# The last batch's first expert layer as plain products, and the kernel's last product in two column halves

## The chip, the core and the metric

The kernel runs on one core of a Trainium2 chip. The metric is device time in microseconds (us). The engines are PE (matrix products; its weight loads are listed as PEld), DVE (vector), ACT (scalar), POOL and SP, which issues most of the transfers. Products are added up in PSUM; GpSimd (POOL) does not touch PSUM here, so what it works on has first been moved to SBUF by DVE or ACT.

## The reference

Sinkhorn attention over 4 batches of 8 heads (768 tokens, head width 64, 8 blocks of 96 tokens) feeds a merged expert layer with 4 experts.

```python
P = sort_net                                   # (batch, head, 8, 8)
for _ in range(5):
    P = P - max(P, -1); P = exp(P); P /= sum(P, -1); P /= sum(P, -2)
k_sorted, v_sorted = P @ blocks of k, P @ blocks of v
attn = softmax(q_b @ k_sb.T / 8)               # inside each block of 96 tokens
x = (attn @ v_sb) laid out as (3072 tokens, 512)

p = domain_probs / sum(domain_probs, -1)       # (3072, 4)
for e in range(4):
    h = relu(x @ w1[e])                        # w1: 512 x 1024
    out += p[:, e] * (h @ w2[e])               # w2: 1024 x 512
```

## The kernel before

The program is written out for one core in a fixed order (`manual_schedule`): each engine's instructions stand in the order in which the lines below issue them, and semaphores are put in from the reads and writes of tiles. The four batches are worked off one after the other. While the expert layers of batch b run on PE, the attention stages of batch b + 1 (`st_q`, `st_v`, `st_k`, `st_s`, `st_a`, `st_x`) are put between them: `slot()` is called after each block of products, and a table (`PLAN`, L602; `PLAN0` for batch 0) says which stage goes into which slot of which chunk.

A batch has 768 tokens, worked on in 3 chunks of 256 (two tiles of 128 tokens). Each chunk has two layers.

- First layer, plain form (`chunk_first`, L733): for each of 4 experts and 2 halves of the 1024 hidden columns, 16 products with 256 token columns (4 output blocks by 4 contraction blocks) fill one PSUM tile of 128 x 1024. One DVE instruction (L748) takes the relu, multiplies by the expert weight `pb` and writes `Hb`. Between these, `h_sums` (L720, additions at L725 to L731) forms sums of blocks of `Hb` in `Sb` on DVE.
- Second layer (`chunk`, L757): seven block products p1 to p7 instead of eight, each 16 products with 256 columns over all experts (`product`, L771). They are read out on ACT and DVE and added on DVE and POOL into the tiles `oa` and `ob`, which SP stores to `out`. The product p3 comes last (L810, then the store of `oa`).

In the batch 3, which is the last, the first layer has another form in the kernel before. `last_chunk` (L1037) takes the place of `chunk`. For each expert, `seven` (L970) forms seven block products with 128 token columns, of 8 matmuls each (`product`, L978 to L981), with partial sums kept in PSUM banks X, Z and Q. It needs sums of weight blocks (`input_sums`, L913; 16 DVE instructions at L919, put into slots of batch 2 by `PLAN_A`, L1122), sums of token blocks (`token_sums`, L923; L935), ACT copies out of PSUM (L1001, L1008, L1016), a relu on ACT (L993) with a multiplication on POOL (L994), and DVE additions (L1017, L1025, L987). Blocks of the next chunk's first expert (`last_begin`, L1032) are put beside the last products of the chunk before. `last_banks` (L939) closes the two PSUM pools of the earlier batches, opens new ones, and issues one 512-column product (L948) on each occasion.

To make room for the weight sums, the attention inputs, the two spread matrices and `vo` lie in one tile, `arena` (L100), of which views are used; the temporary tiles of `seven` lie in buffers that the attention no longer needs.

At the end of the last chunk, p7 is read out by DVE (L1111), POOL and DVE complete `ob` (L1112, L1113), SP stores `ob` (L1114), DVE adds p3 (L1115), and SP stores the last half of `oa` (L1117). The first half of `oa` was stored earlier, after p2 (L1093).

Of the kernel before, what the change touches and what calls it, by code (L numbers as in the profile page):

```python
# [9 lines left out]
F32 = mybir.dt.float32  # L10
# [7 lines left out]
def kernel(  # L18
# [11 lines left out]
    nc = tc.nc  # L30
# [26 lines left out]

    openM, openA = [ctx.enter_context(ExitStack()) for _ in range(2)]
    psM = openM.enter_context(tc.tile_pool(name="psM", bufs=2, space=bass.MemoryType.PSUM))
    psA = openA.enter_context(tc.tile_pool(name="psA", bufs=2, space=bass.MemoryType.PSUM, side="right"))  # L60
# [36 lines left out]

    NW = 4 * R * D
    NQ = NPB * R * 2 * D
    arena = const.tile([P, 4 * NW + NQ + 4 * 4 * P + R * 4 * VW], F16, name="arena")  # L100

# [3 lines left out]
    def load_natural(b, nm, qd):  # L105
        src = {"k": k, "v": v}[nm]
        t = arena[:, ds(("k", "v").index(nm) * 2 * NW + qd * NW, NW)].rearrange("p (h r d) -> p h r d", h=4, r=R)
        natural[(b, nm, qd)] = t
        nc.gpsimd.dma_start(
            t.rearrange("p h r d -> p h (r d)"),  # L110
            src[b, ds(4 * qd, 4)].rearrange("h (p r) d -> p h (r d)", r=R),
        )

    def load_queries(b, heads=range(H)):

        if (b, "q") not in natural:
            natural[(b, "q")] = arena[:, ds(4 * NW, NQ)].rearrange("p (n t h d) -> p n t h d", n=NPB, t=R, h=2)
        t = natural[(b, "q")]
        for h in heads:
            nc.gpsimd.dma_start(t[:, h // 2, :, h % 2, :], q[b, h].rearrange("(t p) d -> p t d", p=P))  # L120
# [64 lines left out]
    kTs, ETs, vs0s, wide = [], [], [], []  # L185
# [4 lines left out]
    for n in range(4):  # L190
        ET = const.tile([P, S + 32], F16, name=f"ET_{n}")
        nc.gpsimd.memset(ET[0:BLK, ds(S, 32)], 0.0)
        ETs.append(ET[0:BLK])
        wide.append(ET)
# [4 lines left out]
    vo = arena[:, ds(4 * NW + NQ + 4 * 4 * P, R * 4 * VW)].rearrange("p (r h w) -> p r h w", r=R, h=4)  # L199
# [122 lines left out]
    def build_PI(eng, n, which):  # L322
        r4 = Rs[:, ds(4 * n, 4), :]
        if which == "k":
            PIk[n] = arena[:, ds(4 * NW + NQ + n % 2 * 4 * P, 4 * P)].rearrange("p (g i c) -> p g i c", g=4, i=NB)
# [6 lines left out]
        else:  # L332
            PIv[n] = arena[:, ds(4 * NW + NQ + (2 + n % 2) * 4 * P, 4 * P)].rearrange("p (g c i) -> p g c i", g=4, i=NB)
# [15 lines left out]
    def st_v(b, pr):  # L349
# [13 lines left out]
        if pr % 2:  # L363
            qd = pr // 2
            vs = att.tile([P, NB, 4, VW], F16, name=f"vs_{b}_{qd}", tag="vs")[0:BLK]
# [63 lines left out]
    def st_a(b, pr):  # L429
        xsl = att.tile([P, NB, 2, D], F16, name=f"xsl_{b}_{pr}", tag="xsl")[0:BLK]  # L430
# [109 lines left out]
    def h_a(qd, qq, ps=None):  # L540
# [11 lines left out]
        if qq not in xsls0:  # L552
            xsls0[qq] = att.tile([P, 2, 4, 2, D], F16, name=f"xsl0_{qq}", tag="xsl")[0:BLK]
# [203 lines left out]
    def chunk(b, c, slot, done=()):  # L757
# [7 lines left out]
        nxt = (b, c + 1) if c + 1 < R // 2 else (b + 1, 0)  # L765
        pbs[nxt] = load_p(*nxt)
# [4 lines left out]
        def product(n, lhs, rhs, pool=psm):  # L771
            ps = pool([P, DH], F32, f"ps_{n}_{b}_{c}")
            for e in es:
                if pool is last_bank and e == 2:
                    last["e0"][6]()
# [15 lines left out]
        if b:  # L791
# [5 lines left out]
            slot()  # L797
            nc.scalar.copy(p5[:], product("p5", sm(0), "t1"))
# [11 lines left out]
            tt(oa2, product("p3", sm(3), "b22", last_bank if last else psm), oa2, ALU.add)  # L810
# [26 lines left out]
        def last_adds(u3):  # L837
            gtt(ob2, u3, ob2, ALU.add)
            tt(ob1, ob1, u3, ALU.add)
# [4 lines left out]
        if c == 0:  # L844
# [21 lines left out]
            last_adds(u3[:])  # L866
            f4()
            store(1, ob)
        else:
# [18 lines left out]
            last_adds(u3[:])  # L888
# [4 lines left out]

    AW = 2 * KH * P

    def a_block(n):
        return arena[:, ds(n * AW, AW)].rearrange("p (k f) -> p k f", k=2)  # L900


    A_ORDER = (3, 4, 5, 10, 11, 0, 1, 2, 6, 7, 8, 9)
    As = []
    for e in range(E):
        w, hk, hf = w1sb[e], NKC // 2, FF // 2
        As.append({
            "a11": w[:, 0:hk, 0:hf], "a12": w[:, hk:NKC, 0:hf],
            "a21": w[:, 0:hk, hf:FF], "a22": w[:, hk:NKC, hf:FF], "s4": w[:, 0:hk, hf:FF],
            "s1": a_block(A_ORDER[3 * e]), "s3": a_block(A_ORDER[3 * e + 1]), "s2": a_block(A_ORDER[3 * e + 2]),  # L910
        })

    def input_sums(e, n):  # L913
        a = As[e]
        dst, x, y, op = (
            ("s1", "a21", "a22", ALU.add), ("s3", "a11", "a21", ALU.subtract),
            ("s2", "s1", "a11", ALU.subtract), ("s4", "a12", "s2", ALU.subtract),
        )[n]
        nc.vector.tensor_tensor(a[dst], a[x], a[y], op)  # L919

    Bs = {}

    def token_sums(c):  # L923

        b = B - 1
        xT = xTs[b].rearrange("p k i x -> p k (i x)")
        blk = lambda k, t: xT[:, ds(2 * k, 2), ds((2 * c + t) * P, P)]
        t3 = kTs[c % 2][:, 0:3 * 2 * P].rearrange("p (n k x) -> p n k x", n=3, k=2)
        t = Bs[c] = {
            "b11": blk(0, 0), "b12": blk(0, 1), "b21": blk(1, 0), "b22": blk(1, 1),  # L930
            "t1": t3[:, 0], "t2": t3[:, 1], "t3": t3[:, 2],
            "t4": wide[c % 2][:, 0:2 * P].rearrange("p (k x) -> p k x", k=2),
        }
        for dst, x, y in (("t1", "b12", "b11"), ("t2", "b22", "t1"), ("t3", "b22", "b12"), ("t4", "b21", "t2")):
            nc.vector.tensor_tensor(t[dst], t[x], t[y], ALU.subtract)  # L935

    last = {}

    def last_banks(n):  # L939

        (openA, openM)[n].close()
        pool = ctx.enter_context(tc.tile_pool(name=f"ps7_{n}", bufs=1, space=bass.MemoryType.PSUM, side=("right", "left")[n]))
        for nm, m in (("X", 1), ("Z", 1), ("Q", 2)):
            last[nm] = last.get(nm, []) + [
                pool.tile([P, 512], F32, tag=f"{nm}{i}", name=f"ps_{nm}{n}{i}") for i in range(m)
            ]

        nc.tensor.matmul(last["X"][n][:], w1sb[0][:, 0, 0:P], w1sb[0][:, 1, 0:512], start=True, stop=True)  # L948

    def prepare_last():  # L950

        last_banks(0)
        last["n"] = 1
        t = moe.tile([P, NKC, NB, BLK], F16, name="tmp7", tag="xT").rearrange("p k i x -> p (k i x)").bitcast(F32)
        room = [t[:, ds(n * 512, 512)] for n in range(3)]
        for m in range(2):
            t = att.tile([P, NB, 4, VW], F16, name=f"tmp7_{m}", tag="vs").rearrange("p i h w -> p (i h w)")
            t = t[:, 0:2048].bitcast(F32)
            room += [t[:, 0:512], t[:, 512:1024]]
        t = att.tile([P, NB, 2, D], F16, name="tmp7_2", tag="xsl").rearrange("p i h d -> p (i h d)").bitcast(F32)  # L960
        room.append(t)
        for n, nm in enumerate(("u2", "u3", "t22", "t12")):
            last[nm] = room[2 * n:2 * n + 2]

    def last_bank(shape, dtype, name):
        n = last["n"]
        last["n"] += 1
        return last["Q"][2 - n % 2][:, 0:shape[1]]

    def seven(c, e):  # L970

        b = B - 1
        a, t, pb = As[e], Bs[c], pbs[(b, c)]
        X, Z, u2, u3, t22, t12 = [last[nm][e % 2] for nm in ("X", "Z", "u2", "u3", "t22", "t12")]
        X, Z, Q = X[:], Z[:], last["Q"][e][:]
        tt = nc.vector.tensor_tensor

        def product(dst, lhs, rhs, first=False):  # L978
            for f in range(KH):
                for k in range(2):  # L980
                    nc.tensor.matmul(  # L981
                        dst[:, ds(f * P, P)], a[lhs][:, k, ds(f * P, P)], t[rhs][:, k, :],
                        start=(first and f == 0 and k == 0), stop=(f == KH - 1 and k == 1), skip_group_check=True,
                    )

        def finish(i, j, src):
            nc.vector.scalar_tensor_tensor(  # L987
                out=Hb[:, e, ds(i * KH, KH), ds(j * P, P)], in0=src.rearrange("p (f x) -> p f x", f=KH), scalar=0.0,
                op0=ALU.max, in1=pb[:, ds(e, 1), ds(j * P, P)].broadcast_to([P, KH, P]), op1=ALU.mult,
            )  # L990

        def finish2(i, j, src):
            nc.scalar.activation(src, src, AF.Relu, bias=0.0, scale=1.0)  # L993
            nc.gpsimd.tensor_tensor(  # L994
                Hb[:, e, ds(i * KH, KH), ds(j * P, P)], src.rearrange("p (f x) -> p f x", f=KH),
                pb[:, ds(e, 1), ds(j * P, P)].broadcast_to([P, KH, P]), ALU.mult,
            )

        def p1():
            product(Z, "a11", "b11", True)  # L1000
            nc.scalar.copy(X, Z)  # L1001

        def p5():
            product(Q, "s1", "t1", True)

        def p6():
            product(X, "s2", "t2")
            nc.scalar.copy(u2, X)  # L1008
# [287 lines left out]
```

## Time and profile before

| what | value |
|---|---|
| median of 3 runs | 369.53 us (369.51 to 370.15) |
| the profiled execution's own time | 369.51 us |
| its span (first to last instruction) | 367.7 us |
| outside the span | 1.81 us |
| PE busy | 358.5 us, 97% |
| DVE busy | 277.5 us, 75% |
| ACT and POOL busy | 121.5 and 118.6 us |
| granted TensorE clock | 1.0 |

Busy time of PE counts a matmul from its start to its modelled end. Matmuls overlap in that count, so the time that one takes in a stream is read from the starts of a row of equal ones and not from the mean duration. In the timeline, a line merges instructions that follow each other: start, length, engine, line, operation, tiles and shape, count, and in brackets the idle time before it and what ended it.

### The profile page before, as it was taken

The page shows a single profiled execution, that of the slowest core. Times are in us where ns is not written, and L with a number is a line of the kernel's source. Part 1 is how long each engine was busy: PE and PEld are TensorE (multiplying, and loading weights), DVE is VectorE, ACT ScalarE, POOL GpSimd, SP SyncE. Part 2 cuts the span into 40 slices and gives each one's busy share as a digit, 9 for nine tenths or more (in the row PEclk, how much of TensorE's full clock was granted, in tenths as well). Part 3 has the DMA queues.
Part 4 walks back from the last instruction along what each step waited for, and adds up shares of the span by engine and source line. Part 5 has one row for each costly group of instructions (what it writes and reads, how often), then busy time and mean ns, then how long its engine had stood idle before and what let it go on. Part 6 is the DMA issues. An engine that isn't in the chain of part 4 may idle for free.

```text
span 367.7 us, 9859 instructions
## 1 busy us (share of the span) xinstructions
PE 358.5 (97%) x4229; PEld 313.8 (85%) x4229; DVE 277.5 (75%) x521; ACT 121.5 (33%) x217; POOL 118.6 (32%) x146
## 2 busy tenths in 40 slices
PE   8799999999999999999999999999999999999996
PEld 8685858879889888898898888998888998998985
DVE  5654898766888774696695685698899879789695
ACT  2664330444230334222100235322011381561740
POOL 8872101713836403000921000100200283282471
PEclk9999999999999999999999999999999999999999
DMA  8999999996996768832795223604204102102101
GB/s 115 207 207 230 209 209 198 199 167 101 175 191 133 107 96 106 170 59 66 109 58 79 87 61 64 152 10 80 78 2 81 58 3 59 59 2 60 60 17 43
DMA packets 69752, 38.31 MB, mean 104 GB/s; under 512 B 40390, under 2 KB 64716, under 8 KB 69708
## 3 DMA queue, kind: packets, MB, share of 16 engines
q0 software_dynamic: 34640, 17.83, 37.3%
q1 hardware_dynamic: 35068, 19.85, 26.8%
q8 instruction: 33, 0.54, 0.6%
q14 instruction: 11, 0.09, 0.1%
HBM read 42.00 MB, written 6.34 MB: 131 GB/s over the span
## 4 chain that ended last, share of the span: by engine, by line
PE 80%; DMA 11%; DVE 5%; POOL 1%; issue 1%; ACT 1%; DVEq 0%; ACTq 0%
PE ps_h L742 28%; PE ps_p L777 23%; PE ps_Q L1069 8%; PE ps_X L981 4%; DMA w<-in_moe_w_dram 4%; DMA xT<-xsl 3%; PE ps_Q L981 3%; PE ps_Z L981 3%; PE ps_o L682 3%; DMA qT<-arena 2%; DMA arena<-in_q_dram 2%; PE ps_h L647 1%; PE ps_s L405 1%; DVE Sb L725 1%; PE ps_a L437 1%
## 5 line engine op out<-in xcount | busy, mean ns | idle before, releaser
L742 PE MATMUL ps_h<-xT,w 128*128 128x256 f16 x1056 | 121.0, 273 | 0.0
L742 PEld LDWEIGHTS <-w 128*128 128x128 f16 x1056 | 102.1, 98 | 13.1
L748 DVE SCALAR_TENSOR_TENSOR Hb<-ps_h,pb 128x1024 f16<-128x1024 f32 x66 | 80.7, 1223 | 29.5 <-PE ps_h L742 29.0
L777 PEld LDWEIGHTS <-Sb 128*128 128x128 f16 x528 | 50.9, 98 | 6.9 <-issue 0.3
L777 PEld LDWEIGHTS <-Hb 128*128 128x128 f16 x396 | 38.1, 98 | 4.6
L804 POOL TENSOR_TENSOR oa<-u,p 128x256 f32<-128x256 f32 x6 | 4.9, 809 | 103.9 <-issue 89.1
L994 POOL TENSOR_TENSOR Hb<-tmp,pb 128x512 f16<-128x512 f32 x24 | 30.9, 1293 | 20.2 <-ACT tmp L993 19.0
L395 ACT CAST kT<-ps_k 64x384 f16<-64x384 f32 x48 | 22.7, 473 | 38.2 <-PE ps_k L386 37.3
L412 ACT ACTIVATE ET<-ps_s 96x768 f16<-96x768 f32 x24 | 18.0, 802 | 46.2 <-PE ps_s L405 46.2
L777 PE MATMUL ps_p<-w,Hb 128*128 128x256 f16 x264 | 31.6, 273 | 0.0
L777 PE MATMUL ps_p<-T,Sb 128*128 128x256 f16 x264 | 31.1, 273 | 0.0
L777 PE MATMUL ps_p<-w,Sb 128*128 128x256 f16 x248 | 29.9, 273 | 0.1
L120 POOL DMA_DIRECT2D arena<-in_q_dram x24 | 19.9, 853 | 12.1 <-DMA w<-in_moe_w_dram 9.7
L981 PEld LDWEIGHTS <-w 128*128 128x128 f16 x384 | 23.3, 98 | 0.4
L725 DVE TENSOR_TENSOR Sb<-Hb 128x512 f16<-128x512 f16 x45 | 22.5, 511 | 0.0
L1069 PEld LDWEIGHTS <-Sb 128*128 128x128 f16 x192 | 18.3, 98 | 3.4 <-issue 0.9
L727 DVE TENSOR_TENSOR Sb<-Sb,Hb 128x512 f16<-128x512 f16 x45 | 18.3, 416 | 0.4
L729 DVE TENSOR_TENSOR Sb<-Hb 128x512 f16<-128x512 f16 x45 | 18.1, 418 | 0.0
L422 DVE TENSOR_TENSOR xsl<-ps_a,rz 96x512 f16<-96x512 f32 x24 | 16.5, 687 | 1.4 <-DMA xT<-xsl 0.6
L981 PEld LDWEIGHTS <-arena 128*128 128x128 f16 x288 | 17.4, 98 | 0.1
L731 DVE TENSOR_TENSOR Sb<-Hb,Sb 128x512 f16<-128x512 f16 x45 | 16.6, 425 | 0.0
L993 ACT ACTIVATE tmp<-tmp 128x512 f32<-128x512 f32 x24 | 15.2, 635 | 3.2 <-DVE tmp L1025 2.6
(173 smaller groups left out, 514.9 us busy)
## 6 DMA issues: line engine op xcount, KB each, us to landing
w<-in_moe_w_dram POOLq DMA_DIRECT2D x7, 1024.0 KB, 27.0
pb<-p_dram SPq DMA_DIRECT2D x12, 512.0 KB, 5.1
arena<-in_k_dram POOLq DMA_DIRECT2D x8, 384.0 KB, 7.9
arena<-in_v_dram POOLq DMA_DIRECT2D x8, 384.0 KB, 8.8
vs<-arena SPq DMA_DIRECT2D x36, 66.0 KB, 4.5
arena<-in_q_dram POOLq DMA_DIRECT2D x24, 96.0 KB, 6.5
out_dram<-ob SPq DMA_DIRECT2D x9, 256.0 KB, 2.2
out_dram<-oa SPq DMA_DIRECT2D x8, 256.0 KB, 2.3
```

Source lines behind the costliest of these rows:

```text
L120: nc.gpsimd.dma_start(t[:, h // 2, :, h % 2, :], q[b, h].rearrange("(t p) d -> p t d", p=P))
L395: nc.scalar.copy(kT[ds(D * hh, D), r], pk[ds(D * r, D), hh].rearrange("p a (i c) -> p a i c", c=CP),)
L412: nc.scalar.activation(ETs[2 * (pr % 2) + hh][:, 0:S].rearrange("c (a x) -> c a x", a=2), pss[hh][0:BLK, :, 0:HS], AF.Exp, bias=0.0, scale ...
L725: tt(sm[0], blk(0, 1), blk(1, 1), ALU.add)
L727: tt(sm[1], sm[0], blk(0, 0), ALU.subtract)
L729: tt(sm[2], blk(0, 0), blk(0, 1), ALU.subtract)
L742: nc.tensor.matmul(ps[:, f, :], w1sb[e][:, kc, ds((4 * g + f) * P, P)], xT[:, kc, ds(2 * c * P, 2 * P)], start=(kc == 0), stop=(kc == NKC ...
L748: nc.vector.scalar_tensor_tensor(out=Hb[:, e, ds(4 * g, 4), :], in0=ps[:], scalar=0.0, op0=ALU.max, in1=pb[:, ds(e, 1), :].broadcast_to([P ...
L777: nc.tensor.matmul(ps[:], lhs(e, f), Ts[e][rhs][:, f, :], start=(e == es[0] and f == 0), stop=(e == E - 1 and f == KH - 1),)
L981: nc.tensor.matmul(dst[:, ds(f * P, P)], a[lhs][:, k, ds(f * P, P)], t[rhs][:, k, :], start=(first and f == 0 and k == 0), stop=(f == KH - ...
L994: nc.gpsimd.tensor_tensor(Hb[:, e, ds(i * KH, KH), ds(j * P, P)], src.rearrange("p (f x) -> p f x", f=KH), pb[:, ds(e, 1), ds(j * P, P)].b ...
L1069: nc.tensor.matmul(ps, lhs(e, f), Ts[e][rhs][:, f, :], start=(e == 0 and f == 0), stop=(e == E - 1 and f == KH - 1),)
```

## The change

In the kernel after, the last batch goes through `chunk` like batches 1 and 2, without attention stages between, since no batch follows. `seven`, `last_chunk`, `input_sums`, `token_sums`, `last_banks`, `prepare_last`, `last_begin` and `PLAN_A` are gone, and with them `arena`: attention inputs, spread matrices and `vo` are tiles of their own again. The loads of batch 1's k, v and q are called some lines earlier in the program; on POOL they stand at the same place among the other instructions.

In the last chunk of the last batch, the first half of `oa` is stored after p2, as before. The last product p3 is formed in two halves of 128 output columns: 16 matmuls into a PSUM tile of the one pool, a DVE addition of 128 columns and a store issued by SP; then 16 matmuls into a tile of the other pool, a DVE addition and a store issued by ACT. The 128 KB store of the last half of `oa` becomes two of 64 KB.

```diff
-    openM, openA = [ctx.enter_context(ExitStack()) for _ in range(2)]
-    psM = openM.enter_context(tc.tile_pool(name="psM", bufs=2, space=bass.MemoryType.PSUM))
-    psA = openA.enter_context(tc.tile_pool(name="psA", bufs=2, space=bass.MemoryType.PSUM, side="right"))
+    psA = ctx.enter_context(tc.tile_pool(name="psA", bufs=2, space=bass.MemoryType.PSUM))
+    psM = ctx.enter_context(tc.tile_pool(name="psM", bufs=2, space=bass.MemoryType.PSUM))
+    nat = ctx.enter_context(tc.tile_pool(name="nat", bufs=2))
...
-    arena = const.tile([P, 4 * NW + NQ + 4 * 4 * P + R * 4 * VW], F16, name="arena")
...
-        t = arena[:, ds(("k", "v").index(nm) * 2 * NW + qd * NW, NW)].rearrange("p (h r d) -> p h r d", h=4, r=R)
+        t = nat.tile([P, 4, R, D], F16, name=f"nat_{nm}_{b}_{qd}", tag=f"nat_{nm}")
...
-            natural[(b, "q")] = arena[:, ds(4 * NW, NQ)].rearrange("p (n t h d) -> p n t h d", n=NPB, t=R, h=2)
+            natural[(b, "q")] = nat.tile([P, NPB, R, 2, D], F16, name=f"natq_{b}", tag="natq", bufs=1)
...
-        nxt = (b, c + 1) if c + 1 < R // 2 else (b + 1, 0)
-        pbs[nxt] = load_p(*nxt)
+        if (b, c) != (B - 1, R // 2 - 1):
+            nxt = (b, c + 1) if c + 1 < R // 2 else (b + 1, 0)
+            pbs[nxt] = load_p(*nxt)
...
+            parts = 2 if (b, c) == (B - 1, R // 2 - 1) else 1
+            if parts == 2:
+                nc.sync.dma_start(o[:, 2 * c, 0:DH], oa1)
             nc.scalar.copy(p5[:], product("p5", sm(0), "t1"))
...
             nc.sync.dma_start(o[:, 2 * c + 1, :], ob[:])
-            tt(oa2, product("p3", sm(3), "b22", last_bank if last else psm), oa2, ALU.add)
+            if parts == 2:
+                for n in range(2):
+                    ps = (psm, psa)[n]([P, DH // 2], F32, f"ps_p3_{b}_{c}_{n}")
+                    cols = ds(n * DH // 2, DH // 2)
+                    for e in es:
+                        for f in range(KH):
+                            nc.tensor.matmul(
+                                ps[:], sm(3)(e, f), Ts[e]["b22"][:, f, cols],
+                                start=(e == es[0] and f == 0), stop=(e == E - 1 and f == KH - 1),
+                            )
+                    tt(oa2[:, cols], ps[:], oa2[:, cols], ALU.add)
+                    eng = (nc.sync, nc.scalar)[n]
+                    eng.dma_start(o[:, 2 * c, ds(DH + n * DH // 2, DH // 2)], oa2[:, cols])
+                return
+            tt(oa2, product("p3", sm(3), "b22"), oa2, ALU.add)
...
-    def input_sums(e, n):
-    def token_sums(c):
-    def last_banks(n):
-    def prepare_last():
-    def seven(c, e):
-    def last_begin(c):
-    def last_chunk(c):
-    PLAN_A = [
...
     for b in range(B):
-        if b == B - 1:
-            for c in range(R // 2):
-                last_chunk(c)
-            break
         plan = PLAN if b else PLAN0
```

## The prediction, made before the changed kernel had run

> **What bounds the kernel now.** I read the page's head first, then the timeline of PE in the last two batches, then a table of stages, then DVE beside PE, and the end last.
>
> The page's head says that PE is busy nearly throughout, at the full granted clock, and that the chain that ended last is PE's.
>
> ```profile
> PE 358.5 (97%) x4229; PEld 313.8 (85%) x4229; DVE 277.5 (75%) x521; ACT 121.5 (33%) x217; POOL 118.6 (32%) x146
> PEclk9999999999999999999999999999999999999999
> PE 80%; DMA 11%; DVE 5%; POOL 1%; issue 1%; ACT 1%; DVEq 0%; ACTq 0%
> ```
>
> So the change is a matter of how many PE steps there are, how long one takes, and how long PE waits between them. The timeline of PE in batch 1 gives the step of a plain first-layer matmul (256 columns), that of batch 3 the step of a block product (128 columns).
>
> ```profile
> 151.18 7.15 PE L742 MATMUL ps_h<-xT,w 128*128 128x256 f16 x64
> 158.16 0.50 PE L386 MATMUL ps_k<-arena 128*128 128x128 f16 x6
> ...
> 316.29 0.61 PE L981 MATMUL ps_X<-kT,arena 128*128 128x128 f16 x8
> ...
> 325.67 1.47 PE L1069 MATMUL ps_Q<-w,Hb 128*128 128x256 f16 x12
> ```
>
> From 151.18 to 158.16 there are 64 steps: 6.98/64 = 109.06 ns. Between 316.29 and 325.67 the timeline has 21 groups of 8: 9.38/168 = 55.83 ns. A block product has half the columns and takes 51% of the time, although each has a weight load of its own.
>
> The table of stages has the stretch from and to, its length, then busy time (and count) of PE, PEld, DVE, ACT and POOL, clock, DMA. Rows one to three are the chunks of batch 1, four to six those of batch 2, seven to nine those of batch 3.
>
> ```profile
> 117.58:147.35 29.77, 29.77 (x311) 26.00 (x308) 20.48 (x34) 10.96 (x19) 8.73 (x10) 1.00 0.74 104
> 147.35:175.74 28.39, 28.39 (x302) 25.38 (x300) 21.02 (x38) 6.40 (x13) 2.47 (x4) 1.00 0.49 93
> 175.74:202.98 27.24, 27.24 (x274) 24.25 (x272) 19.36 (x34) 2.62 (x5) 11.99 (x14) 1.00 0.73 83
> 202.98:232.75 29.77, 29.77 (x311) 26.01 (x309) 19.62 (x35) 10.96 (x19) 1.71 (x2) 1.00 0.30 73
> 232.75:261.14 28.39, 28.39 (x303) 25.41 (x300) 23.92 (x44) 6.40 (x13) 1.51 (x3) 1.00 0.36 71
> 261.14:287.00 25.86, 25.86 (x259) 22.78 (x257) 23.25 (x42) 2.62 (x5) 1.31 (x2) 1.00 0.27 57
> 287.00:312.31 25.31, 25.21 (x340) 23.48 (x337) 21.21 (x43) 12.36 (x23) 12.06 (x11) 1.00 0.14 43
> 312.31:337.39 25.08, 24.93 (x338) 23.37 (x336) 20.93 (x42) 12.38 (x23) 11.81 (x11) 1.00 0.13 43
> 337.39:364.39 27.00, 26.85 (x354) 24.84 (x351) 21.75 (x42) 12.38 (x23) 12.83 (x12) 1.00 0.07 27
> ```
>
> The third row is the model of a chunk after the change: 240 plain steps are 240 x 0.10906 = 26.17 us, and the rest, 1.07, is the two attention stages in it (st_s 0.45, st_a 0.49) and 0.13 of gaps, most of it at st_s. In batch 3 these stages do not exist.
>
> **The change part by part.**
>
> *First layer of batch 3.* Removed are 3 chunks x 4 experts x 7 products x 8 = 672 steps of 55.83 ns, 37.52 us. Added are 3 x 128 = 384 steps of 109.06 ns, 41.88 us. On PE alone that is +4.36 us, all on the path, as PE's chain is the one that ends last.
>
> *What goes with the block products.* PE waits after p4 in each chunk of batch 3, for the late sums: 16 steps from 305.01 end at 306.76 and p5 starts at 307.02; the like from 330.06 to 332.11 and from 355.14 to 357.20. The three waits are 0.26 + 0.30 + 0.31 = 0.87 us. The two 512-column products at L948 take 0.21 us each by the starts around them, 0.42. I make the sum by whole stretches, so that small gaps count too. Before: from 261.14, the start of batch 2's last chunk, to 364.39, where p3 ends, is 103.25 us. After: that chunk as batch 1's, 27.24; three chunks of 26.17, 78.52; the drain of the last matmul behind its step, 0.16 as before (273 - 109 ns, 219 - 56 ns); and p3 in halves, 32 x 55.83 - 16 x 109.06 = 41 ns more. That is 105.96 us, so PE ends 2.71 us later. The terms named give 4.36 + 0.04 - 0.87 - 0.42 = 3.11; the 0.4 left are short gaps between the blocks and the DVE stall in the sixth row.
>
> *DVE in batch 2.* The 16 weight sums (L919, 0.68 us each, 10.9 us of DVE) and the token sums leave. Rows one and four, and two and five, are the same length to 0.01 us, with and without such sums; they lay beside PE and their removal is worth nothing there. Only the sixth row may have lost some 0.15 to them, which the stretch above contains.
>
> *Can DVE keep up with plain chunks without attention stages between?* The DVE timeline of batch 1's last chunk answers that. Each expert has two evictions (L748) and three block sums against 32 PE steps, 3.49 us.
>
> ```profile
> 183.48 1.23 DVE L748 SCALAR_TENSOR_TENSOR Hb<-ps_h,pb 128x1024 f16<-128x1024 f32 x1 [0.74 <-PE ps_h L742]
> 184.62 0.42 DVE L727 TENSOR_TENSOR Sb<-Sb,Hb 128x512 f16<-128x512 f16 x1
> 184.96 0.42 DVE L729 TENSOR_TENSOR Sb<-Hb 128x512 f16<-128x512 f16 x1
> 185.29 1.22 DVE L748 SCALAR_TENSOR_TENSOR Hb<-ps_h,pb 128x1024 f16<-128x1024 f32 x1
> 186.43 0.42 DVE L725 TENSOR_TENSOR Sb<-Hb 128x512 f16<-128x512 f16 x1
> ```
>
> From start to start an eviction with two sums takes 1.81 and one with one sum 1.14 + 0.33 = 1.47, together 3.28, and the next eviction (186.98) starts only when PE has finished its tile. An eviction is at most 0.07 late, and the tile has some 0.2 us to spare before PE wants it again. So I take no stall: 0, with 0.2 per chunk as the upper bound (the gap in the sixth row, 25.86 against 224 x 0.10906 + 0.94 + 0.21, is 0.28). In batch 3, POOL does nothing during the first layer, so it adds no contention. ACT's queue holds three copies per chunk. On SP, `load_p` stands as in batches 1 and 2, needed a second layer (12.2 us) later and landing in 5.1.
>
> *The end.* After p3 the path is: DVE addition, issue, landing, closing.
>
> ```profile
> 363.19 0.99 DVE L1113 TENSOR_TENSOR ob<-ob,u 128x256 f32<-128x256 f32 x1
> 364.25 0.33 SPq L1114 DMA_DIRECT2D out_dram<-ob  x1
> 364.50 0.42 DVE L1115 TENSOR_TENSOR oa<-ps_Q,oa 128x256 f32<-128x256 f32 x1 [0.30 <-PE ps_Q L1069]
> 364.95 0.33 SPq L1117 DMA_DIRECT2D out_dram<-oa  x1
> ```
>
> The addition of the first half can't start when its matmuls end, since DVE still works on `ob` (L1113) until some 0.2 us before p3 ends; the first half saves nothing by itself, and it is done, at about 364.5, as the second half's matmuls end. Its store stands behind that of `ob` on SP, 0.33, and nobody waits for it. The last addition has 128 columns: 256 take 0.42 and 512 take 0.69 (L1017), so 0.29 by the line through both, bounded by 0.20 (a reciprocal of 8 columns, L421) and 0.42. That saves 0.13. The last store moves to ACT, which has nothing queued behind and no DMA of its own in the trace: I take SP's 0.33, bounded above by SP's slow issues (0.58). It lands in 1.7 us at 128 KB, and the 8 KB load of `sort_net` also takes 1.7, so half the bytes save nothing; from 256 to 128 KB it fell from 2.0 to 1.7, so the bound is -0.3. The `ob` store goes out 0.7 before the last and lands 0.4 before it, so it does not take over. The end is worth -0.1, between -0.4 and +0.3.
>
> *Tiles instead of `arena`.* Instruction order is the same on every engine up to the last batch, sums apart. Waits differ in one place: the first query load of a batch waits for all transposes of the old queries instead of those of its own head. They are long done (at 96.77 seven of these loads go out without a pause). Worth 0; I allow 0.4 to either side, as the three runs of one program lie 0.64 us apart.
>
> **Sum.** 369.51 + 2.71 - 0.1 = 372.1 us. The profiled execution is 0.02 below the median, so no correction follows.
>
> **A rule against this.** In the trace a 128-column step with its weight load takes 55.83 ns. The Trainium skill (TensorE: Matmul & The Clock Gate, Back-to-back issue gap) says that a stream of pairs of weight load and matmul is paced by both, at about 81 ns for 128 columns. By that figure the 672 steps would have taken 54.4 us and their removal would make the kernel some 14 us faster (an estimate from that page). The measured step decides here.
>
> **The rivals.**
>
> - *DVE becomes the bound of the plain first layer.* By mean durations an expert costs DVE 2 x 1.223 + 3 x 0.418 = 3.70, against 3.49 on PE: 0.21 x 12 = 2.5 us more, 374.6 us. Against it speak the starts above, which overlap. Chance 0.08.
> - *Faster: the shared tile held up loads.* In the chain, DMA has 40 us: 1.7 and 14.7 at the head, and 24 between 69 and 99 us, through the load of q (L120) and two transposes. If separate tiles let loads of k, v and q start earlier, these parts could shrink; from 3.4 us on (2.6 lost and 0.74) the kernel gets faster. A quarter of the 16.4 at the head would give 372.1 - 4.1 = 368.0. Against it: the loads keep their place on POOL's queue, behind the weight loads that they wait for (9.7 and 8.5 us at L120 and L109), and between 69 and 99 us PE itself idles for them 0.85 and 0.47 us only. Chance 0.03.
> - *No difference.* If the halves at the end brought the whole landing forward (1.7 us) and the gaps another 0.3, some 370 us. The last bytes still leave after the last matmul. Chance 0.03.
>
> **How the numbers follow.** The forecast has 0.86. Its own ends: below, the end at -0.4 instead of -0.1 and the tiles at -0.4, which is 371.4; above, the end at +0.3 instead of -0.1 and three stalls of 0.2, which is 373.1. What is left out, 0.14, lies mostly above. About 0.2%, 0.74 us, can be told from no change here. Slower by that: 0.94; within it 0.03; faster 0.03.
>
> **What would show it.** Each chunk of batch 3 should take 26.2 us (between 26.1 and 26.4), with a step of 109 ns at the first layer's line, and no gap before p5. Batch 2's last chunk should take 27.2. The two last additions should be near 0.29 us each, the second store should come from ACT, and from the last matmul's end to the span's end it should be 3.2 us instead of 3.3. I am wrong if DVE's evictions show no idle time before them and PE waits at the first layer's line, or if batch 3 does not start at 288.4.

## The result, and the profile after

The kernel after takes 374.01 us (median of 4 executions, 373.49 to 375.28) against 369.52 us (median of 4), a ratio of 1.0125 with a 95% interval of 1.0095 to 1.0155. The direction was forecast. The time was not: it lies 1.9 us above the forecast and 0.9 us above the upper end of the range.

The profiled execution is the longest of the four, 375.28 us with a span of 373.4. First the page's head: PE's rows, its clock in 40 slices, and the shares of the chain that ended last.

```profile
PE 364.3 (98%) x3955; PEld 316.3 (85%) x3955; DVE 260.4 (70%) x470; ACT 87.8 (24%) x157; POOL 86.2 (23%) x122
PEclk9999999998999999999999999999999999999999
PE 87%; DMA 8%; POOL 2%; issue 1%; DVE 1%; ACT 0%; DVEq 0%; ACTq 0%; POOLq 0%
```

PE bounds the kernel still. One slice of the clock is below 9; it comes back further down. Next the table of stages, with the columns as in the prediction: the chunks of batches 1, 2 and 3.

```profile
120.37:150.13 29.76, 29.76 (x311) 26.00 (x309) 20.49 (x34) 10.97 (x19) 8.76 (x10) 1.00 0.71 107
150.13:178.52 28.39, 28.39 (x303) 25.39 (x300) 21.01 (x38) 6.41 (x13) 2.47 (x4) 1.00 0.50 91
178.52:205.76 27.24, 27.24 (x275) 24.26 (x273) 19.36 (x34) 2.62 (x5) 11.99 (x14) 1.00 0.69 83
205.76:235.52 29.76, 29.76 (x311) 26.01 (x309) 19.51 (x34) 10.97 (x19) 1.45 (x2) 1.00 0.27 73
235.52:263.91 28.39, 28.39 (x302) 25.39 (x300) 21.01 (x38) 6.41 (x13) 1.45 (x2) 1.00 0.30 71
263.91:291.15 27.24, 27.24 (x275) 24.25 (x272) 19.35 (x34) 2.62 (x5) 1.45 (x2) 1.00 0.26 54
291.15:317.35 26.20, 26.20 (x243) 23.48 (x240) 17.73 (x30) 1.12 (x3) 1.45 (x2) 1.00 0.12 42
317.35:343.55 26.20, 26.20 (x243) 23.48 (x240) 17.74 (x30) 1.12 (x3) 1.45 (x2) 1.00 0.12 41
343.55:369.95 26.40, 26.40 (x258) 23.70 (x255) 17.94 (x31) 1.12 (x3) 1.45 (x2) 1.00 0.07 26
```

From the start of batch 1 on, every row is as forecast: 27.24 for batch 2's last chunk, 26.20 for a chunk of batch 3, PE busy without a gap. From 263.91 to the end of p3 at 369.95 it is 106.04 us; forecast were 105.96, and 103.25 before. What was not forecast stands in the first number: batch 1 starts at 120.37 and not at 117.58. All that is before it is called the head here. By it batch 3 starts at 291.15 and not at 288.4, one of the prediction's signs of being wrong.

The end, from the timeline:

```profile
368.00 1.95 PE L813 MATMUL ps_p<-w,Sb 128*128 128x128 f16 x32
369.69 0.59 DVE L817 TENSOR_TENSOR oa<-ps_p,oa 128x128 f32<-128x128 f32 x2
369.83 0.33 SPq L805 DMA_DIRECT2D out_dram<-ob  x1
370.21 0.42 SPq L819 DMA_DIRECT2D out_dram<-oa  x1
370.36 0.37 ACTq L819 DMA_DIRECT2D out_dram<-oa  x1
```

The last addition takes 0.28, as forecast (0.29), but from the end of p3 to the end of the span it is 373.4 - 369.95 = 3.45 us; before it was 367.7 - 364.39 = 3.31.

So of the 5.7 us between the two spans 2.77 lie between batch 1's start and p3's end, 0.14 at the end, and 2.79 ahead of batch 1. In the head PE's timeline shows where a part of that is. Before:

```profile
82.19 0.51 PE L405 MATMUL ps_s<-qT,kT 64*128 64x96 f16 x16 [0.85 <-DMA qT<-arena]
82.64 1.92 PE L742 MATMUL ps_h<-xT,w 128*128 128x256 f16 x16
```

After:

```profile
83.90 0.51 PE L398 MATMUL ps_s<-qT,kT 64*128 64x96 f16 x16 [2.14 <-DMA qT<-natq]
84.35 2.79 PE L735 MATMUL ps_h<-xT,w 128*128 128x256 f16 x16
```

PE waits 2.14 us instead of 0.85 for the transposed queries of batch 1's second pair of heads, and the 16 first-layer products behind that wait take 2.79 us instead of 1.92. The row of the 3.4 us from 85.20 on has a granted clock of 0.50:

```profile
85.20:88.60 3.40, 3.40 (x30) 2.71 (x29) 1.43 (x2) 0.75 (x2) 0.00 (x0) 0.50 0.80 77
```

This slow stretch belongs to the execution that was profiled (its mean granted clock is 0.993, that of the other three 1.0). The later head is there without it too, as follows.

### The profile page after: what moved, and what is told of

Read it like the earlier page. It is cut to its first block, busy times and chain, and to the rows that moved or that the text cites. A ratio compares the mean times of both kernels' runs of the same rounds, so it can differ in the third digit from the quotient of the medians.

```text
span 373.4 us, 9110 instructions
## 1 busy us (share of the span) xinstructions
PE 364.3 (98%) x3955; PEld 316.3 (85%) x3955; DVE 260.4 (70%) x470; ACT 87.8 (24%) x157; POOL 86.2 (23%) x122
## 4 chain that ended last, share of the span: by engine, by line
PE 87%; DMA 8%; POOL 2%; issue 1%; DVE 1%; ACT 0%; DVEq 0%; ACTq 0%; POOLq 0%
PE ps_h L735 40%; PE ps_p L769 35%; DMA w<-in_moe_w_dram 4%; PE ps_o L675 3%; PE ps_h L640 3%; DMA qT<-natq 2%; DMA natq<-in_q_dram 2%; PE ps_a L430 2%; PE ps_s L398 1%; PE ps_k L379 1%; PE ps_v L346 1%; POOL nat_k L103 0%; POOL nat_v L103 0%; PE ps_s L522 0%; POOL oacc L845 0%
## 5 line engine op out<-in xcount | busy, mean ns | idle before, releaser
L735 PE MATMUL ps_h<-xT,w 128*128 128x256 f16 x1440 | 164.2, 273 | 0.0
L735 PEld LDWEIGHTS <-w 128*128 128x128 f16 x1440 | 140.1, 98 | 17.6
L741 DVE SCALAR_TENSOR_TENSOR Hb<-ps_h,pb 128x1024 f16<-128x1024 f32 x90 | 110.1, 1223 | 41.5 <-PE ps_h L735 39.9
L769 PEld LDWEIGHTS <-Hb 128*128 128x128 f16 x540 | 52.4, 98 | 6.3
L769 PE MATMUL ps_p<-w,Hb 128*128 128x256 f16 x360 | 43.5, 274 | 0.0
L769 PE MATMUL ps_p<-T,Sb 128*128 128x256 f16 x360 | 42.1, 273 | 0.0
L769 PE MATMUL ps_p<-w,Sb 128*128 128x256 f16 x344 | 41.3, 273 | 0.1
L114 POOL DMA_DIRECT2D natq<-in_q_dram x24 | 19.9, 852 | 12.4 <-DMA w<-in_moe_w_dram 9.9
L769 PE MATMUL ps_p<-T,Hb 128*128 128x256 f16 x180 | 21.6, 272 | 0.0
L352 ACT CAST vo<-ps_v 128x768 f16<-128x768 f32 x12 | 9.5, 801 | 20.2 <-PE ps_v L346 12.0
```

Source lines behind the costliest of these rows:

```text
L735: nc.tensor.matmul(ps[:, f, :], w1sb[e][:, kc, ds((4 * g + f) * P, P)], xT[:, kc, ds(2 * c * P, 2 * P)], start=(kc == 0), stop=(kc == NKC ...
L741: nc.vector.scalar_tensor_tensor(out=Hb[:, e, ds(4 * g, 4), :], in0=ps[:], scalar=0.0, op0=ALU.max, in1=pb[:, ds(e, 1), :].broadcast_to([P ...
L769: nc.tensor.matmul(ps[:], lhs(e, f), Ts[e][rhs][:, f, :], start=(e == es[0] and f == 0), stop=(e == E - 1 and f == KH - 1),)
```

## The experiments

Two theories stood at first. **T**: the separate tiles, which the prediction priced at nothing, make the head later. **P**: any kernel with a plain last batch has it (by the length or place of its program, or by the order of its transfers), whatever the tiles. A third possibility was chance: a profile is one execution. Each kernel below was timed beside the kernel before; times are medians in us, and the ratio is to the kernel before in the same series of executions.

| kernel | time (range, executions) | ratio (95%) | batch 1 starts in its profile |
|---|---|---|---|
| after, again | 374.67 (373.18 to 375.25, 6) | 1.0144 (1.0118 to 1.0170) | 118.53 |
| before, again | 369.57 (368.80 to 370.31, 12) | 0.9987 (0.9971 to 1.0003) | 117.48 |
| after, p3 whole | 374.22 (373.67 to 374.67, 5) | 1.0118 (1.0097 to 1.0139) | 119.05 |
| shared tile, plain last batch | 373.73 (372.03 to 374.05, 6) | 1.0099 (1.0077 to 1.0122) | 118.53 |
| the same, a second time | 372.62 (372.04 to 373.73, 6) | 1.0080 (1.0064 to 1.0095) | 117.01 |
| with work tiles of their own | 372.70 (371.93 to 374.28, 6) | 1.0076 (1.0062 to 1.0090) | 119.23 |
| with natural q, k, v of their own | 373.75 (372.82 to 375.51, 6) | 1.0116 (1.0095 to 1.0137) | 119.95 |
| with natural q of its own | 373.51 (373.44 to 375.20, 5) | 1.0115 (1.0084 to 1.0145) | 118.19 |
| with natural k, v of their own | 373.52 (372.18 to 374.61, 6) | 1.0097 (1.0064 to 1.0129) | 119.47 |
| after, a third time | 373.70 (372.88 to 374.54, 5) | 1.0109 (1.0092 to 1.0125) | 118.08 |

### Chance or program

The kernel after, unaltered:

> The changed kernel once more, unaltered. The last batch went as forecast (26.20 us a chunk); the excess of 1.4 to 3 us lies before 100 us, where the profile shows PE waiting 2.14 us at st_s for a q transpose (0.85 before) and one 3.4 us stretch at half clock after it. Theory T (the later head belongs to the new program: tiles in place of the shared arena move addresses and the timing of loads): 373.5 to 374.3 again, with PE's wait at st_s 1.7 us or more. Rival C (chance: both kernels' heads vary alike): some of the rounds fall to 372.0 to 372.5 and the wait at st_s in this profile is near 0.85.

And the kernel before, unaltered:

> The kernel before, unaltered, for a second profile of its head. Four profiles of plain last batches show PE waiting 1.7 to 2.2 us at st_s for the second q transpose, one of them with the head's instructions exactly those of before. Theory P (the head follows the whole program, such as where it lies in memory): the wait is near 0.85 again, landing of the q load 5.9 us after its issue and the transpose 7.1. Rival C (chance): the wait is 1.5 us or more in this profile too, and the time of that run is 370.2 or more.

374.67 and 369.57 us: the difference is the program's, not chance. But one profile of a head is worth little. The kernel before again, which needs no longer, shows a wait of 1.46 us at the same place, between what the two theories expected, and its times spread over 1.5 us.

The lowered clock comes back as well. Half clock over 3.4 of some 370 us makes a mean granted clock of 0.995 (an estimate from the row above). Of the 15 executions of the kernel after in all its series, four are at 0.993 to 0.995, with a mean of 375.14 us, and eleven at 1.0, with a mean of 373.75. Of the 72 executions of the kernel before beside these experiments, five are at 0.995 or less.

### The end: halves or whole

```diff
-            parts = 2 if (b, c) == (B - 1, R // 2 - 1) else 1
+            final = (b, c) == (B - 1, R // 2 - 1)
+            parts = 1
...
-            nc.sync.dma_start(o[:, 2 * c, :], oa[:])
+            if final:
+                nc.sync.dma_start(o[:, 2 * c, DH:Dm], oa2)
+            else:
+                nc.sync.dma_start(o[:, 2 * c, :], oa[:])
```

> The changed kernel with the last product undivided: 16 matmuls of 256 columns, one addition, one 128 KB store on SP. The prediction gives the halves 0.1 us, so 0.1 us slower than the changed kernel, between 0.4 slower and 0.3 faster. If the store on ACT were what costs the excess, this one would be 1 us or more faster.

374.22 us against 374.67 for the halves in the same series, and 3.37 us from the end of p3 to the end of the span against 3.47: the halves and the store from ACT bring nothing that can be measured. The end is not the cause of the miss.

### Where the queries are loaded

Since PE waits for transposed queries, three kernels moved their loads or transposes. The first loads the second pair of heads three slots earlier (in the kernel after):

```diff
-        (0, 9, st_v, 0), ... (0, 11, st_k, 0), (0, 11, st_n, 1), (1, 0, st_q, 1),
+        (0, 8, st_n, 1), (0, 9, st_v, 0), ... (0, 11, st_k, 0), (1, 0, st_q, 1),
```

> The changed kernel with the load of the second pair of q heads (st_n 1) three slots earlier, so that on POOL it stands ahead of the two additions that wait for ACT, some 5 us earlier. If PE's wait for the q transpose at st_s is what makes the head late, it goes (2.1 us in the profile of after, or 1.3 us more than before), and the kernel takes 371.7 to 372.4. If the load only queues longer behind the weight loads (DMA engines full until 72 us), the wait shrinks by less than 0.5 us and the time stays at 373.5 or more.

373.77 us (372.77 to 375.51), ratio 1.0112 (1.0086 to 1.0138): no gain that can be told from the spread, and not the 371.7 to 372.4 expected. In its profile the wait moves to the scores before, 2.75 us at 75.3, and 1.03 are left at 85.1.

The second takes load and transposes of the last pair out of the crowded stretch, in the kernel after and, for comparison, in the kernel before:

```diff
-        (1, 4, st_n, 3), ... (1, 9, st_q, 3),
+        (1, 7, st_n, 3), ... (2, 0, st_q, 3),
```

> The changed kernel with the last pair of q heads of batch 1 loaded later: on POOL behind the addition that waits for ACT at 87 us instead of at 73 to 75, its transpose moved from slot (1, 9) to (2, 0). If the second q transpose is late because four q loads run beside it (7.5 us in place of 3.7), it takes 6.5 us or less and PE's wait at st_s falls below 1.2 us: 372.2 to 373.2. If the load before it is what makes it late (6.5 us behind the weight loads), the wait stays at 1.7 or more and the time at 373.5 or more.

> The kernel before with the same later load of the last pair of q heads. The wait at st_s (0.85) goes if the four loads beside the transpose cause it: 368.4 to 369.0, faster than both kernels. If the moved transpose meets the load of the next batch's queries, which waits for it, 369.4 or a little more.

380.26 us (ratio 1.0256, 1.0226 to 1.0286) and 372.89 us (1.0077, 1.0047 to 1.0108). In the kernel after, with two query loads beside them instead of four, the transposes of the second pair landed in 5.8 us instead of 7.5, and the wait of 2.14 us fell to 0.55, so what runs beside these transfers changes when they land. But the moved transposes are then needed sooner than they land: in the first kernel PE waits 2.66 us at 105.7 and 4.29 at 124.1, in the second 3.16 at 106.8.

### The shared tile kept: a first, misleading answer

This kernel is the one before with the last batch in the plain form and nothing else: up to the last batch its instructions and tiles are those of the kernel before, apart from the weight and token sums and the first block products, which stood in batch 2.

```diff
-        if b == B - 1:
-            for c in range(R // 2):
-                last_chunk(c)
-            break
... (nor the calls of input_sums, prepare_last, token_sums and last_begin in batch 2, nor load_p after the last chunk)
```

> The kernel before with nothing changed but the last batch, which goes through the plain chunk; the shared arena, pools, places of loads and the undivided last product stay. Theory T: the head is that of before, so 372.1 to 372.4, 1.5 us or more below the changed kernel in the same rounds, PE's wait at st_s near 0.85. Rival C: the same as the changed kernel within 0.5 us. A third, D (the change of the last batch itself costs more in timed runs than in the profile): 373.5 or more with a head like before's.

373.73 us, and batch 1 at 118.53 in the profile. I read that as the end of theory T and looked for what any plain kernel shares. That reading was too quick: it rested on one profile and on six times spread from 372.03 to 374.05.

### The length of the program

The plain kernels' programs are shorter. Work behind the end, which no output uses, made the shared-tile kernel as long as the kernel before:

```diff
+    pool7 = psM.tile([P, 512], F32, tag="ps", name="pad_ps")
+    for _ in range(292):
+        nc.tensor.matmul(pool7[0:32, 0:32], ident[:, 0:32], ident[:, 0:32], start=True, stop=True)
... (and 73, 80 and 36 one-column fills or copies on DVE, ACT and POOL)
```

> The shared-arena kernel with the plain last batch, and behind its end 292 tiny products (32 columns), 80 one-element ACT copies, 73 DVE and 36 POOL memsets that compute nothing, so that each engine's program is as long as before's; they take some 8 to 20 us at the end, which is to be taken off. Theory P in the form that program length matters: the wait at st_s falls to near 0.85 and the last batch begins about 1 us earlier in the span than in the kernel without them. Rival C, or any cause other than length: the wait is again 1.7 or more.

Its profile had batch 1 at 117.55, as before; so the same was done to the kernel after (with 276 products), in full and in parts, and the kernel before was cut short:

```diff
-            for c in range(R // 2):
+            for c in range(R // 2 - 1):
                 last_chunk(c)
```

> The kernel after, with work behind its end that no output uses: 276 products of 32 x 32 on PE, 73 fills of one column on DVE, 80 one-column copies on ACT, 36 fills on POOL, so that every engine's program has about as many instructions as in the kernel before. Its time is not to be compared, only the start of batch 1's first chunk. Theory L (the length or place of the program in memory sets how the head runs): the head ends as in the kernel before, batch 1 starts at 117.4 to 117.9 us, with PE's wait before the scores of the second half near 1 us, and p3 ends near 366.9 to 367.3 (364.39 + 2.71). Theory C (the head is late for a cause in the changed kernel's own instructions, or by chance of the execution): batch 1 starts at 118.5 to 120.5, and p3 ends at 368 to 370.

> The kernel before without the last chunk of the last batch (rows 2816 to 3071 of the output are left out), which makes its PE program as short as that of the kernel after (7835 instructions instead of 8459; after 7911), while every engine's instructions up to there, and every address, are those of the kernel before. Theory L: batch 1 starts at 118.5 us or later, as in all three kernels with a short program. Theory C: batch 1 starts at 117.4 to 117.9, as in the kernel before. The time should be about 27.0 us (one chunk, 337.39 to 364.39) less than before: by L 343.5 to 346, by C 342.3 to 343.0.

> The kernel after with the 276 products of 32 x 32 on PE behind its end and nothing on the other engines. They take 276 x 25.5 ns = 7.0 us if they start as p3 ends; the store's 3.5 us lie beside them. If PE's program length alone decides (a part of theory L), batch 1 starts at 117.4 to 117.9 as in the kernel before; if the other engines' programs decide or nothing does, 118.5 to 120.5.

> The kernel after with the fills and copies on DVE, ACT and POOL behind its end and nothing on PE. If the length of these engines' programs decides, batch 1 starts at 117.4 to 117.9; if PE's does or nothing does, 118.5 to 120.5. ACT's 80 copies take some 16 us, so the time itself is 10 to 15 us longer.

The kernel after with all of it starts batch 1 at 118.45, with PE's alone at 121.22, with the rest alone at 120.15; the kernel before, cut, at 117.87, and the spans of its five executions (345.0 to 345.7) lie within 0.7 us. None of these profiles shows that the length of the program is it: the three padded forms of the kernel after keep a late head, and the cut kernel before has an early one. (The padded kernels' times, 383.08, 390.50, 380.40 and 390.86 us, hold the added work. The cut kernel's time, 347.21 us, misses both expectations: 337.39 is where the first products of the cut chunk begin, put between the last ones of the chunk before, whose p3 ends at 340.9 in the cut kernel's trace. That has no bearing on the head.)

### The tiles, settled by many executions

What was left was to time the shared-tile kernel again, in one series with the kernel after and two kernels between them. One has the natural q, k and v in tiles of their own (`nat`, as in the kernel after), the other the spread matrices, `vo` and the 96-row tiles. The edits, one for each kernel:

```diff
-        t = arena[:, ds(("k", "v").index(nm) * 2 * NW + qd * NW, NW)].rearrange("p (h r d) -> p h r d", h=4, r=R)
+        t = nat.tile([P, 4, R, D], F16, name=f"nat_{nm}_{b}_{qd}", tag=f"nat_{nm}")
...
-            natural[(b, "q")] = arena[:, ds(4 * NW, NQ)].rearrange("p (n t h d) -> p n t h d", n=NPB, t=R, h=2)
+            natural[(b, "q")] = nat.tile([P, NPB, R, 2, D], F16, name=f"natq_{b}", tag="natq", bufs=1)
```

```diff
-            PIk[n] = arena[:, ds(4 * NW + NQ + n % 2 * 4 * P, 4 * P)].rearrange("p (g i c) -> p g i c", g=4, i=NB)
+            PIk[n] = att.tile([P, 4, NB, CP], F16, name=f"PIk_{n}", tag="PIk")
... (the same for PIv; vo, ET, vs and xsl as in the kernel after)
```

> The plain last batch with the shared tile kept, unaltered a second time, beside the kernel after and two kernels between them, so that the four heads can be told apart by many executions and not by one profile each. Theory T (the tiles that replace the shared tile make the head later): its head is that of the kernel before, batch 1 starts at 117 to 118.5, and its time is 369.5 + 2.7 + 0.4 = 372.6 us (0.4 for the 256 KB store at the end), 372.0 to 373.2. Theory P (any kernel with a plain last batch has the late head): batch 1 starts at 118.5 to 120.5 and the time is 373.5 to 375.

> As the kernel with the shared tile, but the natural k, v and q of the attention lie in tiles of a pool of their own, as in the kernel after; spread matrices and vo stay in a shared tile. Theory T, if the loads' tiles carry it: time 1 to 2 us over that of the kernel with the shared tile, 373.5 to 375, batch 1 from 118.5 to 120.5 us. Theory T, if the other tiles carry it, or theory P: the same time as the kernel with the shared tile within 0.5 us.

> As the kernel with the shared tile, but the spread matrices, vo and the 96-row tiles (ET, vs, xsl) are those of the kernel after; natural k, v and q stay in the shared tile. Theory T, if these tiles carry it: time 1 to 2 us over that of the kernel with the shared tile. Theory T, if the loads' tiles carry it, or theory P: the same within 0.5 us.

> The kernel after, unaltered, in the same call. Both theories: 373.5 to 375 us, batch 1 from 118.5 to 120.5. Theory T expects it 1 to 2 us over the kernel with the shared tile less 0.25 for the end (their stores differ); theory P expects the two within 0.5 us.

The shared-tile kernel took 372.62 us, where theory T had said 372.6; with work tiles of their own it stays there (372.70), and with natural q, k and v of their own it goes to 373.75, the level of the kernel after (373.70). This last edit is the narrowest one; the means of six executions each are 372.68 and 374.02 us, 1.3 us apart with a 95% interval of 0.2 to 2.5. Over all executions of unaltered kernels, the shared-tile kernel has a mean of 373.05 us (12) and the kernel after 374.12 us (15). The former's end is 0.25 us longer, since it stores all of `oa` (3.7 us from p3 to the span's end), so up to the end of p3 the two differ by 1.07 + 0.25 = 1.32 us, with a 95% interval of about 0.7 to 1.9. Theory T holds, and the first answer of the shared-tile kernel was its spread. A part of the 1.07 is the lowered clock: one of the 12 executions of the shared-tile kernel is at 0.995, and without it and the four of the kernel after the means are 372.96 and 373.75 us, 0.8 apart. One of 12 and four of 15 are too few to show that the longer wait brings it on.

Then q alone and k and v alone:

> As the plain last batch with the shared tile, but the natural q lies in a tile of its own; natural k and v, spread matrices and vo stay in the shared tile. If the tile of q carries the 1.1 us (its loads and transposes are where PE waits), the time is 373.3 to 374.5 us, as with all natural tiles (373.75); if it is the tiles of k and v, 372.2 to 373.0, as with the shared tile (372.62).

> As the plain last batch with the shared tile, but natural k and v lie in tiles of their own; natural q, spread matrices and vo stay in the shared tile. If the tiles of k and v carry the 1.1 us, the time is 373.3 to 374.5; if that of q does, 372.2 to 373.0. If both this kernel and the one with the tile of q stay near 372.6, or both go up, the place of the tiles in SBUF and not their waits is what is left.

373.51 and 373.52 us, both about 0.9 over the shared tile, but in another series and on another chip; by the ratios they are 1.0115 and 1.0097 against 1.0080, and both intervals overlap with its own. By time alone the two can't be told apart. The traces tell more. The transfers of the stretch from 66 to 88 us, medians from issue to landing in the last column; shared tile first:

```profile
vs<-arena SPq DMA_DIRECT2D x12, 66.0 KB, 4.3
arena<-in_q_dram POOLq DMA_DIRECT2D x6, 96.0 KB, 6.3
qT<-arena SPq DMA_TRANSPOSE x3, 6.6
```

The kernel with only q in a tile of its own:

```profile
vs<-arena SPq DMA_DIRECT2D x12, 66.0 KB, 4.8
natq<-in_q_dram POOLq DMA_DIRECT2D x6, 96.0 KB, 7.0
qT<-natq SPq DMA_TRANSPOSE x3, 6.8
```

Not only the loads and transposes of q land later, but those beside them too (`vs`). This pair of profiles shows it more clearly than most: the kernel before, a second time, has 4.8, 7.0 and 6.7 with the shared tile. Over all profiles with q's loads at their usual place, the transposes land in 6.6 or 6.7 us in 7 of the 8 kernels that have q in the shared tile (7.2 in the other), and in 6.8 to 7.2 us in 8 of the 9 that have it in its own (6.3 in the other, which the padding with DVE, ACT and POOL work made). PE's own timeline agrees. The stretch from its start on the first layer at some 70.8 us to its start on the next at some 95.4 has a mean of 25.0 us in the 8 and 26.0 us in the 9 (25.8 without the profile with the lowered clock); its waits for transposed queries in there have means of 1.2 and 2.0 us. The kernel with k and v in their own tiles belongs to the 8 in this (24.89 us, a wait of 1.11): its profile is late by waits of 0.99 and 1.03 us for first weights and values before 21 us, as the one with work tiles is (0.99 at 16.9, 1.13 at 30.1), and whether its longer time is more than spread stays open. So does why these transfers take longer. In the profiles compared, the loads and transposes of this stretch wait for the same things. Where q lies differs, but a move of q alone does not seem to do it: in the kernel with k and v in their own tiles, q begins at the start of the shared tile instead of 4 * NW = 6144 elements into it, and its transposes land in 6.6 us like the others of the 8. And with q out of the shared tile, what lies behind it moves as well.

## Why the prediction was right in its sign and wrong in its size

- *Chunks of batch 3, batch 2's last chunk, no DVE stall.* Right: 26.20, 27.24, and no gap; the stretch is 106.04 against 105.96. Removing DVE sums from batch 2 was worth nothing, as said. The rival of DVE as the bound falls. With 55.83 ns for a 128-column step the +2.71 came out within 0.1 us, so the figure of the Trainium skill (TensorE: Matmul & The Clock Gate, Back-to-back issue gap) that was weighed there, some 81 ns, is not this stream's.
- *The end.* Wrong by 0.25: +0.15 and not -0.1. The addition shrank to 0.28 us as expected, but the store that ends the kernel is no sooner for being split, and it issues in 0.37 on ACT (SP's, for the other half, took 0.42 instead of 0.33).
- *"Tiles instead of `arena`" worth 0, at most 0.4 to either side.* This step failed. It measured +1.32 us (about 0.7 to 1.9), some 0.3 of it in executions with a lowered clock, for which the sum had no term. I looked at the waits and the order of instructions, found them alike, and concluded that the transfers would take as long. They did not. The bound of 0.4 was drawn from the spread of three runs of one program, which says nothing of another placement; and the upper end of the range, 373.1, did not even contain it. With it, 373.5, the result would still lie outside. The trace of before had also shown how little room there was: PE already waited 0.85 us for these transposes, so whatever they lose after that is on the path.
- *"They are long done."* Wrong too. With q in its own tile, the first query load of batch 2 now waits for the last transposes of batch 1, as POOL's timelines show, before and after:

```profile
96.77 5.75 POOL L120 DMA_DIRECT2D arena<-in_q_dram  x7
```

```profile
102.53 6.56 POOL L114 DMA_DIRECT2D natq<-in_q_dram  x8 [2.42 <-DMA qT<-natq]
```

  In all nine kernels with q in its own tile POOL waits before this first load, 2.4 to 6.7 us; in none of the eight with the shared tile. Loads without a pause at one time are no evidence that a coarser wait would be met: the last transposes were issued at 89.6 and took up to 10.3 us. It costs little, since nobody needs these queries soon: PE's stretch from there to batch 1 has a mean of 22.0 us in the 8 profiles and 22.1 in the 9 (23.6 in the one with the wait of 6.7).
- *Sum.* 369.5 + 2.7 + 0.15 + 1.3 = 373.7 us; measured are 374.0 (4 executions) and 374.1 (15). The 0.4 left are those by which the shared-tile kernel, with a mean of 373.05, lies above its own sum, 372.6. No run explains them; they may be spread, or a small cost that all plain kernels share.

The rival that had the tiles matter had the sign the other way round: separate tiles were to free the loads. They did not start sooner, and the ones beside PE's wait landed later.

## What to carry to other kernels

Where PE already waits a little for a transfer, every change to that transfer's buffers belongs into the sum, even when order and waits stay as they are; its bound comes from how far the landing times of such transfers vary, not from the spread of one program. Replacing views of one tile with a tile of its own also made the wait of the first writer coarser here, so look when the last reader ends. And a difference of about 1 us in a stage that varies by 1 us from execution to execution is settled by many executions of two kernels side by side, not by one profile of each: here one profile and six times led to the wrong theory for eight experiments.

## What the runs showed of the hardware

- Transfers in the same stretch with the same sizes and order took 5 to 11% longer to land when q lay in a tile of its own (medians over the 8 and 9 profiles: transposes 6.6 and 6.9 us, query loads 6.45 and 7.1, `vs` 4.6 and 5.1; single profiles of the two groups overlap). I had expected no effect, and can't explain it.
- One wait of PE of 2.14 us was followed by some 3.4 us at a granted clock of 0.50, which cost 1.6 us more (from the scores' start to the second group of p products it is 89.53 - 83.90 = 5.63 us, before 86.19 - 82.19 = 4.00), so the wait was not the whole price. But the length of the wait alone does not decide it. Waits of 1.81 and 1.87 us at the same place (q alone in its own tile; the kernel after, a third time) were followed by a clock of 1.00, and so were longer ones: 2.21 us (the kernel after, again), 2.75 (early query load) and 3.16 (the kernel before with late queries). The Trainium skill (TensorE: Matmul & The Clock Gate, Part 1: The HAM clock gate) puts the drop behind an idle window of some 3.4 us; in this trace a wait shorter than that was enough.
